# A fused attention and FFT-mixing kernel on one core: its instruction list laid out with other durations, and three small moves of work

## The chip, the cores and the metric

The kernel runs on one core of one Trainium2 chip. The metric is device time in microseconds from launch to end; a profiled execution has a span of its own, from the first to the last instruction. A core has the engines TensorE (PE in the profile), VectorE (DVE), ScalarE (ACT), GpSimd (POOL) and SyncE (SP, which here issues all transfers).

## The reference

For 8 batches of 8 heads: 32 global queries attend to all 544 keys, 512 local queries attend to the 32 global keys and to local keys at most 32 away. The result `x` (8 x 544 x 512) goes through a mixing layer with two weights, 512x2048 and 2048x512:

```python
X = np.fft.fft(np.fft.fft(x, axis=1), axis=2)
u = x + np.real(X)
un = (u - mu) / np.sqrt(var + 1e-06)       # over the last axis
out = u + np.maximum(un @ w_ch1, 0.0) @ w_ch2
```

The inputs are float32 and the weights come as 64-bit floats' bits. All products are made of float16 high and low parts (three matmuls for one product).

## The kernel before

**A list made by a planner.** All work is a list of jobs. `jobs_...` methods add jobs to a `Plan`: an engine, an estimated duration in us, a method that emits the instructions, what it reads and writes, and perhaps a due time `t`. `Plan.targets` gives the other jobs due times backwards from their successors; `Plan.run` simulates five engines, at each step starting on an engine the ready job with the earliest due time. `emit` then writes the instructions in that order. On the chip each engine takes its own in order and waits for semaphores, so the estimates change nothing but the order. Buffers are rings (`X` 3, `uh` 2, `ph` 3, `pl` 3, `h` 3, `ps1` 2, `acc0`, `acc1`, `un`, `lw` 1) and a pool of four PSUM banks; the order of the list decides who gets a free one.

**The weights.** 32 tiles are loaded (`w_load`, L401); POOL (or ACT, each `ALOW`-th) makes a piece of the low bits (`w_low`, L417, L415), ACT scales the high word (`w_split64`, L408), DVE joins them (`w_size`, L421, and `w_sign`, L435), TensorE adds up magnitudes by block (`w_sum`, L431, into `acc0` or `acc1`), DVE takes a maximum of each block of four tiles (`w_max`, L441) and a power of two as scale. Then `w_hi` (ACT, L471) makes the float16 high part and `w_lo` the low part: on DVE in one instruction (L464), or, for the tile numbers in `LOP`, on POOL in two (L461, L462). `W_AT`, `W_PACE`, `W2_AT`, `S_AT`, `S2_AT` and so on are due times.

**Attention.** A batch has four pairs of heads `p`, a pair four units `u`. A pair's `load` and `load_v` may start at `hold` (`L_HOLD` for batches after the first) and, with `queue`, when the simulated transfer queue is nearly empty. `sums` and `sums_v` (ACT, L520) are block sums for a scale; `z_total`, `z_scale` follow. `prep_...`, `v_...` split queries, keys and values into high and low parts. Then for each unit: `scores` (PE, L616), `masked` (DVE, L624), `exps` (ACT, L631), `p_hi` (ACT, L635), `p_lo` (POOL, L640), `turn` (SP, a DMA transpose, L645), `values` (PE, L661, L664), and `norm` for two units (DVE, L675 to L677), which writes `X`. `U_AT`, `B_AT` and `APER` are the due times of a pair's scores in `unit_at`; `EARLY` is the number of pairs with early estimates for PE.

**The DFT of a batch.** DVE and POOL fold rows and columns (`d_odd`, `d_even`, `d_even2`, `d_odd2`, L808 to L847, `d_tail` on POOL), ACT and DVE split the result (`d_hi`, L855, `d_lo`, L859, `d_tail_hi`, `d_tail_lo`, L882), `d_first` is the first DFT (PE, L905; five tiles, for batch 0 in the PSUM tiles that `SPARE` names), `d_z`, `d_z2` split again, `d_second` (L940) is the second DFT, and `d_add`, `d_addc` (DVE, L966, L957), `d_as`, `d_tadd` (L972, L977 to L980) add it to `X`.

**The FFN.** 17 chunks of 256 rows, two halves `j` each. Before a chunk: `l_bn`, `l_v` (DVE statistics), `l_un` (DVE, L1019, normed rows in float32, tile `un`), `l_hi` (ACT, L1023), `l_lo` (DVE, L1027), `l_turn` (SP, L1033, into `uh`). Then for eight `fp`: `f_first` (PE, L1059, into `ps1`), `f_hi` (ACT, L1064), `f_lo` (DVE, L1068), `f_second` (PE, L1078). FFN matmuls have the latest due times on PE, so that they fill what attention and DFT leave. `l_root` is on POOL. Chunks 13 to 16 run as two pairs (`jobs_duo`) with seven products in place of eight for the first layer (L1207, L1273); POOL and ACT prepare mixed weights for them (`jobs_mixes`, `t_sum`, L1108, to `t_lo`, L1129).

The functions that the change touches:

## Time and profile before

| | |
|---|---|
| time, median of 3 runs | 1028.36 us (1025.35 to 1030.54) |
| the profiled execution | 1025.88 us, span 1024.1 us |
| PE busy | 920.3 us (90%) |
| DVE busy | 733.5 us (72%) |
| ACT busy | 611.5 us (60%) |
| POOL busy | 599.1 us (59%) |
| mean granted TensorE clock | 0.939 |

A busy share is an average over stages that differ; the page cuts the span into 40 slices of 25.6 us, and a table by stage gives each engine's busy time in a stretch that one names. A granted clock of 1.00 is 2.4 GHz, one of 0.50 is 1.2 GHz. Lines (L640) are those of the kernel printed above.

### The profile page before, as it was taken

What the parts mean: (1) busy time and instruction counts of PE and PEld (TensorE: products, weight loads), DVE (VectorE), ACT (ScalarE), POOL (GpSimd) and SP (SyncE); (2) the same over time, 40 slices, a digit from 0 to 9 for tenths busy, and PEclk for the clock granted to TensorE, in tenths of its full rate; (3) what the DMA queues carried; (4) which work ended last, traced back from release to release, by engine and by line L of the source; (5) the groups of instructions that cost most, each with busy time, mean ns of one, the idle gap of its engine ahead of it and who ended that gap; (6) DMA issues with size and microseconds to landing.
All of it is one profiled execution on the core that took longest, in us unless ns stands there. A gap on an engine that the chain in (4) does not pass through costs nothing. (4 is left out here: it accounts for less than half of the span.)

```text
span 1024.1 us, 25350 instructions
## 1 busy us (share of the span) xinstructions
PE 920.3 (90%) x9768; PEld 641.4 (63%) x9768; DVE 733.5 (72%) x1929; ACT 611.5 (60%) x1347; POOL 599.1 (59%) x861
## 2 busy tenths in 40 slices
PE   2354459999999999999999999999999999899996
PEld 1233347667667767676776676677766775566663
DVE  4887999977668756785688567956775678975543
ACT  7996769973687478637864886487446344312210
POOL 6999856872587168616962785476436598711000
PEclk9555569999999999999999999999999999999998
DMA  9899456462575276327752865367226213112001
GB/s 364 250 280 235 110 107 134 105 148 42 129 148 130 46 156 151 87 55 146 136 129 46 142 154 99 84 122 140 41 58 107 55 22 68 39 27 78 1 1 41
DMA packets 227809, 113.10 MB, mean 110 GB/s; under 512 B 202824, under 2 KB 210152, under 8 KB 227688
## 3 DMA queue, kind: packets, MB, share of 16 engines
q1 hardware_dynamic: 227688, 111.49, 48.4%
q8 instruction: 76, 1.25, 0.5%
q14 instruction: 45, 0.37, 0.1%
HBM read 47.37 MB, written 9.44 MB: 55 GB/s over the span
## 5 line engine op out<-in xcount | busy, mean ns | idle before, releaser
L1059 PE MATMUL ps<-uh,wh 128*128 128x256 f16 x2496 | 291.4, 274 | 0.9 <-DMA uh<-unh 0.9
L1078 PE MATMUL acc<-wh,h 128*128 128x512 f16 x1248 | 287.6, 381 | 0.5 <-DVE h L1068 0.5
L1059 PEld LDWEIGHTS <-wh 128*128 128x128 f16 x2496 | 240.8, 98 | 36.3 <-issue 2.0
L1078 PEld LDWEIGHTS <-h 128*128 128x128 f16 x1248 | 116.9, 98 | 129.6 <-issue 2.3
L640 POOL TENSOR_TENSOR ph<-pe,ph 128x448 f16<-128x448 f32 (+1 forms) x128 | 139.9, 1107 | 77.7 <-ACT ph L635 57.4
L1068 DVE SCALAR_TENSOR_TENSOR h<-ps,h 128x512 f16<-128x512 f32 x104 | 71.5, 687 | 102.2 <-ACT h L1064 102.0
L1064 ACT ACTIVATE h<-ps 128x512 f16<-128x512 f32 x104 | 61.6, 592 | 112.0 <-PE ps L1059 111.5
L624 DVE CUSTOM_DVE_ANT_0 pe<-bk,msk,z 128x224 f32<-128x224 f32 (+1 forms) x256 | 102.4, 454 | 24.0 <-PE bk L616 20.7
L631 ACT ACTIVATE pe<-pe,nm 128x224 f32<-128x224 f32 (+1 forms) x256 | 105.0, 476 | 13.1 <-DVE nm L624 12.9
L661 PE MATMUL bk<-vN,pl 128*128 128x65 f16 x768 | 67.0, 201 | 21.9 <-DMA pl<-ph 13.6
L635 ACT ACTIVATE ph<-pe 128x448 f16<-128x448 f32 (+1 forms) x128 | 70.7, 579 | 18.6 <-DMA pl<-ph 17.9
L1039 POOL TENSOR_TENSOR ve<-ve 128x2 f32<-128x2 f32 x17 | 4.3, 255 | 120.8 <-DVE un L1019 99.7
L661 PEld LDWEIGHTS <-pl 128*128 128x128 f16 x768 | 59.4, 103 | 24.1 <-DMA pl<-ph 18.7
L664 PEld LDWEIGHTS <-pl 96*128 96x128 f16 (+1 forms) x768 | 57.4, 103 | 9.8 <-issue 5.7
L616 PEld LDWEIGHTS <-qT 64*128 64x128 f16 x1536 | 49.8, 98 | 21.9 <-issue 18.2
L616 PE MATMUL bk<-kT,qT 64*128 64x192 f16 (+2 forms) x1536 | 57.1, 220 | 6.8 <-POOL kT L600 4.2
L664 PE MATMUL bk<-vB,pl 96*128 96x65 f16 (+1 forms) x576 | 51.6, 202 | 0.0
L431 PE MATMUL wl<-wm,partb 128*128 128x256 bf16 x64 | 18.6, 394 | 32.9 <-DVE wm L421 32.9
L1273 PE MATMUL acc<-wh,h 128*128 128x512 f16 x192 | 46.5, 379 | 1.8 <-DVE h L1260 0.9
L600 POOL TENSOR_TENSOR kT<-qk,kT 128x559 f16<-128x559 f32 x32 | 40.6, 1269 | 12.6 <-ACT kT L595 12.2
L575 POOL TENSOR_TENSOR vN<-vf,vN 128x640 f16<-128x640 f32 x32 | 44.6, 1394 | 5.4 <-ACT vN L571 5.0
L1255 ACT ACTIVATE hb<-ph 128x512 f16<-128x512 f32 x16 | 10.1, 630 | 62.8 <-DVE ph L1240 62.8
(258 smaller groups left out, 1886.7 us busy)
## 6 DMA issues: line engine op xcount, KB each, us to landing
qk<-in_qk SPq DMA_DIRECT2D x32, 535.5 KB
rw<-in_moe_w_ch SPq DMA_DIRECT2D x22, 512.0 KB
vf<-in_v SPq DMA_DIRECT2D x32, 320.0 KB
out<-X SPq DMA_DIRECT2D x13, 512.0 KB
raw<-in_moe_w_ch SPq DMA_DIRECT2D x10, 512.0 KB
vB<-vN SPq DMA_DIRECT2D x32, 97.5 KB
vB<-vN SPq DMA_DIRECT2D x64, 32.5 KB
pl<-ph SPq DMA_TRANSPOSE x128
```

Source lines behind the costliest of these rows:

```text
L616: nc.tensor.matmul(S[h][:, t + w0:t + w1], qT[r, a, j], kT[r, k0:k0 + w1 - w0], start=m == 0, stop=m == 2)
L624: nc.vector.tensor_tensor_reduce(self.per[j][:, h, 0:w], S[h][:, t:t + w], self.msk[:, j, 0:w], z[:, 8:9], 3e38, op0=ALU.add, op1=ALU.min, ...
L631: self.nc.scalar.activation(pe[:, h], pe[:, h], AF.Exp, bias=nm[:, h:h + 1], scale=-1.0)
L635: self.nc.scalar.activation(ph[:, 0, :, 0:WIDE[i % 4]], self.per[i % 4][:, :, 0:WIDE[i % 4]], AF.Copy)
L640: self.nc.gpsimd.tensor_sub(ph[:, 1, :, 0:w], self.per[i % 4][:, :, 0:w], ph[:, 0, :, 0:w])
L661: nc.tensor.matmul(pv[:, j % 2, h], pl[:, 4 * a + 2 * h], vN[:, j, c, h, :], start=m == 0, stop=False)
L664: nc.tensor.matmul(pv[:, j % 2, h], pl[0:n, 4 * a + 2 * h + 1], vb, start=False, stop=m == 2)
L1059: nc.tensor.matmul(ps[:, q], wt[:, w, c0:c0 + P], uh[:, :, 4 * a + kt, :], start=n == 0, stop=n == 11)
L1064: self.nc.scalar.activation(h[:, 0], self.fps[c, fp], AF.Relu)
L1068: self.nc.vector.scalar_tensor_tensor(h[:, 1], self.fps.pop((c, fp)), 0.0, h[:, 0], op0=ALU.max, op1=ALU.subtract)
L1078: nc.tensor.matmul(self.acc_f[c][j], h[:, a, q, j * P:(j + 1) * P], self.w[1, f][:, w, :], start=f == 0 and a == 0 and w == 0, stop=f == 1 ...
L1273: nc.tensor.matmul(self.acc_f[c][j], h[:, a, q, j * P:(j + 1) * P], self.w[1, f][:, w, :], start=first and q + a + w == 0, stop=last and q ...
```

## The change

Estimated durations and due times of many jobs are replaced, so the list has another order. Beside that, this work itself changes: `LOP` is empty, so all `w_lo` are on DVE; `l_hi` makes the high part from `X` with a scale and a bias and not from `un`, and half 1's `un` lies in the tile `lw`; `d_odd2` is cut into `d_odd1` and `d_odd2`; batch 0's first DFT takes other PSUM tiles (`SPARE`); the mixed weights wait for `ht` of batch 7; and three tail jobs of the last batch's DFT get their due times 40 us earlier like the rest (`BOOST`). Loads of later batches are held until 90 in place of 50, scores of later batches are due from 140 at 103 us a batch in place of 150 at 109. `warm` adds no job, since `WARM` is empty.

```diff
...
 PERIOD = 109.0
-U_AT, U_PACE = 9.0, 4.0
-B_AT, B_PACE = 150.0, 5.0
-W_AT, W_PACE = 7.0, 2.6
+U_AT, U_PACE = 12.0, 4.5
+B_AT, B_PACE = 140.0, 5.0
+W_AT, W_PACE = 4.0, 2.2
 W2_AT, W2_PACE = 48.0, 2.6
-S_AT, S_PACE = 25.0, 4.2
-S2_AT, S2_PACE = 190.0, 5.0
+S_AT, S_PACE = 40.0, 3.2
+S2_AT, S2_PACE = 190.0, 4.0
...
 ALOW = 4
-LOP = (1, 3, 5, 7, 9, 11, 13, 15)
-EARLY = 6
-L_HOLD = 50.0
-QUEUE = 4.0
+LOP = ()
+EARLY = 4
+WARM = ()
+L_HOLD = 90.0
+QUEUE = 2.0
...
 LNB = True
-SPARE = {0: "acc0", 1: "acc1", 4: "ps1", 2: "ps1", (0, 0): "acc0", (0, 1): "acc1"}
+SPARE = {0: "ps1", 1: "ps1", 4: "acc0", (0, 0): "acc0", (0, 1): "acc1"}
...
 MATE = {c: (u, n) for u, v in enumerate(PAIRS) for n, c in enumerate(v)}
-APER = 109.0
+APER = 103.0
...
     def emit(self):
+        t0 = min(j.start for j in self.order if j.fn.__name__ == "f_first")
         for j in self.order:
+            if j.fn.__name__ == "warm" and j.start > t0:
+                continue
...

+    def d_odd1(self, b):
+        self.odd_rows(self.nc.vector, self.D[b]["s4"][:, :, P:2 * P])
+
...
         se, s4 = self.nc.vector, self.D[b]["s4"]
-        self.odd_rows(se, s4[:, :, P:2 * P])
...
         L = self.L[c]
-        L["un", j] = un = self.p1.tile([P, DM], F32, name="un", tag="un")
-        L["hl", j] = hl = self.p2.tile([P, 2, DM], F16, name="unh")
+        L["un", j] = un = self.p1.tile([P, DM], F32, name="un", tag=("un", "lw")[j])
...
         L = self.L[c]
-        self.nc.scalar.activation(L["hl", j][:, 0], L["un", j], AF.Copy)
+        L["hl", j] = hl = self.p2.tile([P, 2, DM], F16, name="unh")
+        ve = L["ve"]
+        self.nc.scalar.activation(hl[:, 0], self.u_row(c, j), AF.Identity, scale=ve[:, 1, j:j + 1], bias=ve[:, 2, j:j + 1])
...
             add("ACT", .55, self.w_split64, k, i, r=[raw], w=[w, m], k=x4, t=T + .5)
-            add("DVE", .62, self.w_size, k, i, r=[m, lw], w=[w], t=T + 1.5)
+            add("DVE", .66, self.w_size, k, i, r=[m, lw], w=[w], t=T + 1.5)
...
             add("PE", .52, self.w_sum, k, i, r=[w], w=[wl] + end, t=T + 2)
-            add("DVE", .62, self.w_sign, k, i, r=[m, w], w=[w], t=T + 2)
+            add("DVE", .66, self.w_sign, k, i, r=[m, w], w=[w], t=T + 2)
...
             else:
-                add("DVE", 1.15, self.w_lo, k, i, False, r=[w], w=[h], t=T + 1)
+                add("DVE", .92, self.w_lo, k, i, False, r=[w], w=[h], t=T + 1)
+
+    def warm(self, n):
+        self.nc.tensor.matmul(self.bank(("bank", "wm", n)), self.c1[:, 0, 0, 0:P], self.c2.rearrange("p a b c d -> p (a b c d)")[:, 0:512], start=True, stop=True)
+
+    def jobs_warm(self, add):
+        n = 0
+        for count, us, hold in WARM:
+            for _ in range(count):
+                add("PE", us, self.warm, n, r=[("const",)], w=[("bank", "wm", n)], t=1e6, hold=hold, margin=.1)
+                n += 1
...
                 pe, ph = ("pe", u), ("ph", u)
-                add("DVE", .77, self.masked, u, r=[*S, z, ("msk",), pe], w=[pe, ("nm", u)])
+                add("DVE", .92 if p < 8 else .84, self.masked, u, r=[*S, z, ("msk",), pe], w=[pe, ("nm", u)])
...
                 add("POOL", 1.08, self.p_lo, u, r=[pe, ph], w=[ph])
-                add("SP", 1.45, self.turn, u, r=[ph], w=[("pl", u)], svc=1.0, margin=SPM)
+                add("SP", 1.45, self.turn, u, r=[ph], w=[("pl", u)], svc=1.6, margin=SPM)
...
             add("PE", rate * .85, self.g_scores, g, r=[gT] + kv, w=S + [("pg", g)], t=(U[0] + U[2]) / 2, margin=pem)
-            add("DVE", 1.03, self.g_max, g, r=[*S, zg], w=[("ng", g)])
+            add("DVE", 1.1, self.g_max, g, r=[*S, zg], w=[("ng", g)])
...
     def jobs_dft(self, add, b):
-        rate, pem = (PEF, PEM0) if b == 0 else (1.0, PEM)
+        rate, pem = (1.1, PEM0) if b == 0 else (1.0, PEM0 if b == B - 1 else PEM)
...
             add(eng, us, self.d_odd, b, i, r=src, w=[s4h[i]] + ([] if i else [s4]), k=[X, s4])
-            add("DVE", 3.0 if i else 2.9, self.d_even, b, i, r=src, w=[x4h[i]] + own, k=[X, e4])
-        add("DVE", 1.35, self.d_even2, b, r=x4h, w=x4h, k=[e4])
-        add("DVE", 2.3, self.d_odd2, b, r=s4h, w=s4h, k=[s4], late=6.0)
+            add("DVE", 3.25, self.d_even, b, i, r=src, w=[x4h[i]] + own, k=[X, e4])
+        add("DVE", 1.5 if b else 2.6, self.d_even2, b, r=x4h, w=x4h, k=[e4])
+        add("DVE", 1.3, self.d_odd1, b, r=s4h[1:], w=s4h[1:], k=[s4], late=4.0)
+        add("DVE", .95, self.d_odd2, b, r=s4h, w=s4h, k=[s4], late=5.0)
...
             add("ACT", .63, self.d_hi, b, i, r=[*src, dsc], w=[eh[i]], k=own)
-            add("DVE", .70, self.d_lo, b, i, r=[*src, dsc, eh[i]], w=[eh[i]], k=own)
+            add("DVE", .95, self.d_lo, b, i, r=[*src, dsc, eh[i]], w=[eh[i]], k=own)
         add("ACT", 1.48, self.d_tail_hi, b, r=[et, dsc], w=[ht])
-        add("DVE", 1.10, self.d_tail_lo, b, r=[et, dsc, ht], w=[ht])
+        add("DVE", 1.2 if b else 1.7, self.d_tail_lo, b, r=[et, dsc, ht], w=[ht])
...
         for j in range(2):
-            un, hl = ("un", c, j), ("unh", c, j)
-            add("DVE", .58, self.l_un, c, j, r=r0[j:j + 1] + [ve], w=[un, hl], k=[X], t=L, back=LNB)
-            add("ACT", .55, self.l_hi, c, j, r=[un], w=[hl], t=L, back=LNB)
+            un, hl = (("un", "lw")[j], c, j), ("unh", c, j)
+            add("ACT", .60, self.l_hi, c, j, r=r0[j:j + 1] + [ve], w=[hl], k=[X], t=L, back=LNB)
+            add("DVE", .58, self.l_un, c, j, r=r0[j:j + 1] + [ve], w=[un], k=[X], t=L, back=LNB)
...
     def jobs_mixes(self, add):
-        late = [("xM", 31), ("xgo", 7, 1)]
+        late = [("xM", 31), ("xgo", 7, 1), ("ht", 7)]
...
             self.jobs_duo(add, u)
+        self.jobs_warm(add)
...
             n = j.fn.__name__
-            if n.startswith("d") and j.a[0] == B - 1 and not (n in ("d_second", "d_addc", "d_add") and j.a[1] or n in ("d_tailsec", "d_as", "d_tadd")):
+            if n.startswith("d") and j.a[0] == B - 1 and not (n in ("d_second", "d_addc", "d_add") and j.a[1]):
...
```

## Rows read from the trace of the kernel before

**Rows 1.** The page, 40 slices: busy tenths of TensorE

```profile
PE   2354459999999999999999999999999999899996
```

**Rows 2.** Stage table: busy PE, PEld, DVE, ACT, POOL (count); PEclk, DMA, GB/s

```profile
20.00:110.00 90.00, 44.42 (x592) 30.04 (x591) 73.46 (x198) 79.13 (x170) 83.64 (x92) 0.57 0.93 256
110.00:146.00 36.00, 13.69 (x157) 10.58 (x157) 34.89 (x84) 25.57 (x57) 26.22 (x40) 0.59 0.45 99
...
217.00:221.00 4.00, 1.67 (x32) 1.22 (x23) 0.82 (x3) 1.36 (x5) 3.46 (x5) 0.83 0.96 198
221.00:850.00 629.00, 627.85 (x7038) 442.94 (x7037) 449.19 (x1232) 390.98 (x870) 374.27 (x551) 1.00 0.50 100
850.00:900.00 50.00, 45.06 (x305) 30.18 (x304) 43.31 (x83) 16.79 (x37) 39.19 (x56) 0.97 0.26 60
```

**Rows 3.** Timeline of PE: start, us, line, tile, count, idle before

```profile
145.86 5.28 PE L1059 MATMUL ps<-uh,wh 128*128 128x256 f16 x24 [0.92 <-DMA uh<-unh]
```

**Rows 4.** SyncE's waits, 20 to 110 us: us, times, longest

```profile
SPq L645 <- POOL lw L417: 10.4, 5, 4.4
SPq L645 <- POOL wm L461: 4.7, 4, 2.3
```

**Rows 5.** Groups of POOL by line, 20 to 110 us: busy, mean ns, idle

```profile
L461 POOL TENSOR_SCALAR wm<-wm,wsc 128x512 f32<-128x512 f32 x8 | 13.4, 1673 | 0.5
L462 POOL TENSOR_TENSOR wh<-wm,wh 128x512 f16<-128x512 f32 x8 | 9.7, 1211 | 0.7
```

**Rows 6.** Stage table of DVE's L464 alone

```profile
20.00:110.00 90.00, 6.93 (x8) 0.57 0.93 256
```

**Rows 7.** Timeline of DVE, 24 to 142 us

```profile
24.14 1.15 DVE L464 SCALAR_TENSOR_TENSOR wh<-wm,wsc,wh 128x512 f16<-128x512 f32 x1
...
94.38 2.48 DVE L829 TENSOR_TENSOR e<-e 128x128 f32<-128x128 f32 x1
96.77 0.28 DVE L830 TENSOR_TENSOR e<-e 128x128 f32<-128x128 f32 x1
...
109.78 0.42 DVE L677 TENSOR_TENSOR X<-bk,dn 128x256 f32<-128x256 f32 x1
...
124.37 0.41 DVE L441 TENSOR_REDUCE mx<-wl 128x1 f32<-128x256 f32 x1
...
126.13 0.15 DVE L529 TENSOR_SCALAR wsc<-wsc 128x1 int32<-128x1 int32 x1
...
138.41 0.69 DVE L1027 TENSOR_TENSOR unh<-un,unh 128x512 f16<-128x512 f32 x1
...
141.17 0.68 DVE L1027 TENSOR_TENSOR unh<-un,unh 128x512 f16<-128x512 f32 x1
```

**Rows 8.** Stage table of ACT's L520 alone

```profile
20.00:110.00 90.00, 11.17 (x30) 0.57 0.93 256
```

**Rows 9.** Timeline of POOL, 95 us

```profile
95.45 1.25 POOL L808 TENSOR_TENSOR s<-X 128x508 f32<-128x508 f32 x1
```

**Rows 10.** Timeline of ACT, 137 us

```profile
137.74 0.63 ACT L1023 ACTIVATE unh<-un 128x512 f16<-128x512 f32 x1 [0.32 <-DVE un L1019]
```

**Rows 11.** Timeline of ACT, 219 us

```profile
219.75 0.58 ACT L635 ACTIVATE ph<-pe 128x448 f16<-128x448 f32 x1 [2.64 <-DMA pl<-ph]
```

**Rows 12.** Timeline of PE, 888 to 919 us

```profile
888.79 0.80 PE L1207 MATMUL bk<-pe,tq 128*128 128x256 f16 x3 [2.54 <-DVE xt L980]
...
918.36 2.13 PE L1207 MATMUL bk<-pe,tp 128*128 128x256 f16 x18
```

**Rows 13.** Timeline of DVE, 822 us

```profile
822.05 1.52 DVE L882 SCALAR_TENSOR_TENSOR ht<-et,dsc,ht 32x513 f16<-32x513 f32 x1 [0.93 <-ACT ht L878]
```

**Rows 14.** Timeline of POOL, 813 to 898 us

```profile
813.05 2.50 POOL L1108 TENSOR_TENSOR tf<-wh 128x512 f32<-128x512 f16 x2
...
895.99 1.60 POOL L1129 TENSOR_TENSOR tp<-vf,tp 128x512 f16<-128x512 f32 x1
```

## The prediction

> **What bounds the kernel now.** I read the page's row of TensorE first, then the stage table, then what the slow stage waits for. From the seventh slice on TensorE runs at nine tenths or more in all slices but three near the end [rows 1], and from 221 to 850 us it is busy 627.85 of 629 [rows 2]. So nothing but TensorE sets the length of that stretch, and what DVE, ACT or POOL gain or lose there costs nothing unless it opens a hole. What can be won lies at three places: the start, up to the first layer's first matmuls at 145.86 [rows 3]; a hole at 217 to 221 (4.00 - 1.67 = 2.33 us idle); and 850 to 900 (50 - 45.06 = 4.94 us idle) [rows 2]. Of the start, 20 to 110 us is the attention of batch 0 together with splitting the weights, 110 to 146 its DFT and layer norm.
>
> From 20 to 110 us POOL is the fullest engine, 83.64 of 90 us, against ACT 79.13 and DVE 73.46; the DMA share is 0.93 [rows 2]. That POOL is also the one waited for shows in SyncE's own waits: the transposes of attention probabilities (L645) wait 10.4 us that are put down to POOL's weight pieces (L417) and 4.7 us to the first half of a POOL `w_lo` (L461) [rows 4], and SyncE issues in order, so loads stand behind them. From 110 to 146 DVE is the bound: 34.89 of 36 us [rows 2].
>
> The sum is made against the profiled execution, 1025.88 us (span 1024.1). The median of the three runs, 1028.36, is 2.48 above it; I carry the difference over.
>
> **The change part by part.**
>
> *A. Eight `w_lo` from POOL to DVE.* Removed from POOL: 8 x (1.673 + 1.211) = 23.07 us, all between 20 and 110 [rows 5]; POOL falls to 60.6 of 90. Added to DVE: 8 of L464, 8 x 0.866 = 6.93 us by the mean of the eight that DVE has there already [rows 6], so DVE rises to 80.4. One took 1.15 [rows 7], so 9.2 us is the upper bound. The next limits are then DVE 80.4, ACT 79.1 and the DMA queues, 0.93 x 90 = 83.7. The later loads (hold 50 to 90) push block sums of batch 1 out of this stretch: L520 is 11.17 us in 30 instructions there [rows 8], six a pair, so 2.2 us a pair; the two pairs of batch 0 left need 4.5, and 6.7 us can go. That lowers ACT to about 72.5 and takes the same pairs' loads from the queues. So DVE's 80.4 is the floor. The stretch can shrink by 0 (dependences, not POOL, hold it) to 90 - 80.4 = 9.6 us; I take the middle, **-5**: POOL was packed to 93% with SyncE waiting on it, and DVE will not pack better. Queued behind a `w_lo` on DVE is the next masked-scores instruction, and behind that ACT's exponentials; that is why I don't take the full 9.6.
>
> DVE and POOL do slow each other: L829, 128x128, took 2.48 us and ended at 96.86, just when POOL's 1.25 us L808 of 95.45 was over, while L830 of the same shape took 0.28 right after [rows 7, 9]. The Trainium skill, SBUF — State Buffer, "Who interferes with whom", says that a DVE instruction with two SBUF inputs and a POOL instruction that reads SBUF exclude each other. L464 has two such inputs, so the rule speaks against the move: by it POOL would get back only 23.07 - 6.93 = 16.1 us, which leaves it at 67.5 of 90, still below DVE; the sum would be the same.
>
> *B. Layer norm and the first DFT.* `l_hi` now reads X itself with scale and bias on ACT, in place of waiting for `l_un`; it stays one ACT instruction (0.63 us before [rows 10]) and runs beside `l_un`. For row 1 of a chunk `un` gets a tile of its own. Before, un of row 1 had to wait for lo of row 0 (138.41, 0.69), and lo of row 1 came at 141.17 [rows 7]. With both un early, lo of row 1 can follow at about 139.1: 2.07 us for the second transpose, on which the first matmuls wait; bounds 0 to 2.1, taken 2.0. The first DFT's tiles 0 and 1 go to the first layer's PSUM tiles, off those of the weights' block sums, whose last maximum came at 124.37 in the middle of the DFT; its chain on DVE to the last scale ends at 126.28, 1.9 us [rows 7]. It needn't stand there any more: 0 to 1.9, taken 1.0. One DFT tile more takes one of four banks; the scores of batch 1 that then wait are not urgent. The split of `d_odd2` and the new durations can put the even half's low part ahead of odd work: DVE's total is unchanged, so 0 up to the 1.9 of the same place again, taken 1.0 for TensorE and ACT working earlier beside it. Sum **-4.0** (0 to -5.9).
>
> *C. The hole at 217.* ACT stood 2.64 us before L635 for a transpose [rows 11], the second layer waited behind it, and TensorE's granted clock was 0.83 there [rows 2]. The list now counts 1.6 us of queue for each such transpose in place of 1.0. That may or may not move it: 0 to -2.33, and as much again for the low clock; **-1.5**. Against this, attention asked for sooner (103 in place of 109 us a batch) puts more of it ahead of FFN work; bounded by more such holes of 2.33 us in the later batches, taken nothing, since DVE, ACT and POOL are each under 72% busy from 221 to 850 [rows 2].
>
> *D. The end.* The last batch's tail second step and additions (`d_tailsec`, `d_as`, `d_tadd`) are brought forward. TensorE waited 2.54 us for L980, the last of them, at 888.79 [rows 12], and the stretch's clock was 0.97 for 50 us, 1.5 us more [rows 2]. Early, the bank is free long before: 0 to -4.0, taken **-3**. The mixes on POOL now wait for `ht` of batch 7, which was ready at 823.6 (L882) [rows 13] where the first mix had begun at 813.05: 10 us later. Their last instruction ended at 897.59 [rows 14] and what they make last is first used at 918.36 [rows 12]: 20.8 us of cover, so nothing; with the cover gone it would cost the 10 us.
>
> *Back.* A start 9 us shorter has less room for batch 1's TensorE work, which is then done under load. TensorE was busy 13.69 of 36 us at a clock of 0.59 [rows 2], 0.22 us of full-speed work a us: **+2.0** for A and B's 9 us.
>
> *Nothing:* `warm` (its list is empty); the margins, rates and other estimates, which act through the order alone; `QUEUE` 2 lets loads be issued later, and its cover is a queue that is 0.93 busy [rows 2]; where it drains, a load's wait is A's lower bound, nothing gained.
>
> Sum: -5 - 4 - 1.5 - 3 + 2 = -11.5, so 1025.88 - 11.5 = 1014.4 as a profiled execution, and 1028.36 - 11.5 = **1016.9 us** as the median.
>
> **The rivals.**
>
> 1. *The list moves little.* ACT at 79.1 and the queues at 0.93 were nearly as full as POOL; A gives nothing, B and D half (-3.5), C nothing: about 1025. For it: 73.46 + 6.93 on DVE is only 3 us under POOL's 83.64. Against: SyncE's waits name POOL, not ACT or DVE [rows 4].
> 2. *All covers hold.* A -9.6, B -5.9, C -4.7, D -4.0, back +3.5: -20.7, 1007.7. Against: DVE would have to be packed without a gap from 20 to 110 us.
> 3. *Slower: DVE becomes the bound of the start.* The eight `w_lo` fall due among the masked scores and before the DFT. Once DVE is the engine on which 20 to 110 us ends, each us put on it is a us of the span: 8 x 1.15 = +9.2, B and D at half, -3.5: 1034. It decides from the point where DVE has under 7 us of idle time before the first DFT; it had 16.5 [rows 2].
> 4. *Slower: the steady stretch gets holes.* Attention asked for 6 us a batch sooner stands in the in-order queues of ACT and SyncE ahead of FFN's `f_hi`. A hole like that at 217, with its low clock 3.5 us, in each of seven batches is +24.5, less 11.5: 1041; it turns the sign from four such holes on.
>
> **How the numbers follow.** My forecast (1010 to 1022) 0.50; rival 1, 0.22; rival 2, 0.12; rivals 3 and 4, 0.16 together, a quarter of it near the old time. A measurement here can tell about 0.5% (5.1 us) from no change: faster is under 1023.2, slower over 1033.5. Faster: 0.50 + 0.12 + a small part of rival 1, 0.64. Same: the rest of rival 1 and the quarter, 0.24. Slower: 0.12. The range takes in rivals 1 and 2 with a little beside them and leaves out most of 3 and 4: 1006 to 1031; the likeliest case alone is 1010 to 1022.
>
> **What would show it.** A: no L461 or L462 on POOL; POOL under 75% busy up to the last attention norm of batch 0, and that norm, at 109.78 before [rows 7], ahead of 106. B: the hi rounding beside un, the first matmul of the first layer between 134 and 140. C: TensorE without a hole over 2 us from there to 850. D: no wait for the tail's additions. I am wrong if the first layer still starts at 145 or later (rivals 1, 3), or if TensorE idles more than 5 us in the steady stretch (rival 4).

## The result, and the profile after

The changed kernel takes **1017.92 us** (median of 4 runs, 1017.44 to 1018.22) against 1028.05 for the kernel before (4 runs beside it, 1025.35 to 1030.54): a ratio of 0.9902, 95% interval 0.9876 to 0.9927. The forecast was 1016.9, range 1006 to 1031, likeliest case 1010 to 1022. Its profiled execution took 1017.78 us with a span of 1016.0, against 1025.88 and 1024.1: 8.1 us less, where the sum of the prediction had 11.5. All medians, ranges and ratios here and below leave out one execution of run 10 (3245 us) and one of the kernel before beside runs 5 to 8 (2391 us), which ran in a slow state.

The total came out near the forecast. Its parts did not, and alone, in the old order, none of those tried is worth anything.

The stage table of the changed kernel answers to [rows 2] ("..." marks what is left out). Columns as there: stretch, its length, busy time of PE, PEld, DVE, ACT, POOL, then PEclk, DMA share, GB/s. The second stretch ends where the first layer now begins.

```profile
20.00:110.00 90.00, 44.18 (x588) 30.51 (x587) 84.34 (x206) 76.35 (x163) 68.66 (x83) 0.60 0.89 244
110.00:143.00 33.00, 12.28 (x107) 9.19 (x107) 26.46 (x63) 22.70 (x47) 16.37 (x29) 0.55 0.34 98
143.00:217.00 74.00, 73.88 (x951) 53.24 (x948) 66.46 (x174) 68.12 (x152) 59.13 (x78) 0.99 0.72 134
217.00:221.00 4.00, 4.00 (x32) 2.81 (x30) 3.86 (x8) 2.01 (x4) 4.00 (x5) 1.00 0.64 166
221.00:825.00 604.00, 603.53 (x6920) 430.66 (x6919) 446.51 (x1233) 397.85 (x870) 364.94 (x541) 1.00 0.53 106
221.00:850.00 629.00, 626.59 (x7079) 446.05 (x7078) 470.96 (x1278) 406.54 (x888) 387.76 (x580) 1.00 0.53 105
...
825.00:850.00 25.00, 23.06 (x162) 15.39 (x160) 24.46 (x46) 8.70 (x18) 22.82 (x40) 1.00 0.42 92
...
850.00:900.00 50.00, 45.39 (x309) 29.58 (x308) 44.08 (x75) 16.02 (x36) 35.70 (x53) 1.00 0.23 41
```

Rows of the kernel before are needed beside it that the prediction did not use: its first layer's first 71 us, the 4.3 us behind the hole, and the stretch up to 850 us in two parts.

```profile
146.00:217.00 71.00, 71.00 (x896) 51.35 (x896) 61.51 (x162) 62.38 (x140) 53.77 (x71) 0.96 0.57 127
...
219.70:224.00 4.30, 4.29 (x23) 2.09 (x24) 3.16 (x5) 4.16 (x10) 3.69 (x7) 0.61 0.81 141
221.00:825.00 604.00, 602.85 (x6834) 426.00 (x6832) 428.87 (x1199) 381.78 (x852) 351.34 (x528) 1.00 0.51 103
825.00:850.00 25.00, 25.00 (x206) 16.93 (x205) 20.32 (x34) 9.21 (x19) 22.93 (x24) 1.00 0.12 23
```

Three things are to be seen. In 20 to 110 us POOL fell from 83.64 to 68.66 and DVE rose from 73.46 to 84.34; DVE is now the fullest engine. In 110 to 143 us no engine is full: DVE, the bound of that stretch before (34.89 of 36), is busy 26.46 of 33. And the hole at 217 is gone, with TensorE's granted clock at 1.00 there in place of 0.83 (and of 0.61 from the hole's end to 224), and at 0.99 in place of 0.96 ahead of it.

The timeline of the changed kernel, PE first: the first layer's first matmul is the third row [rows 3].

```profile
119.14 0.42 PE L911 MATMUL dps<-c1r,eh 128*128 128x144 f16 x2 [5.89 <-ACT eh L861]
...
140.18 0.59 PE L459 MATMUL bk<-vac,part 128*128 128x6 f32 x2 [8.03 <-ACT junk L524]
...
143.06 3.11 PE L1066 MATMUL ps<-uh,wh 128*128 128x256 f16 x20
```

DVE, from the last attention norm of batch 0 (L681) to the layer norm's low parts (L1034) [rows 7]:

```profile
105.79 0.42 DVE L681 TENSOR_TENSOR X<-bk,dn 128x256 f32<-128x256 f32 x1
...
117.63 0.75 DVE L888 SCALAR_TENSOR_TENSOR ht<-et,dsc,ht 32x513 f16<-32x513 f32 x1 [5.00 <-ACT ht L884]
...
121.06 0.42 DVE L445 TENSOR_REDUCE mx<-wl 128x1 f32<-128x256 f32 x1
...
136.34 1.00 DVE L1024 TENSOR_SCALAR un<-X,ve 128x512 f32<-128x512 f32 x2
137.26 1.33 DVE L1034 TENSOR_TENSOR unh<-un,unh 128x512 f16<-128x512 f32 x2
```

And ACT in the same stretch; L524 is a block sum of batch 1, L884 and L861 are the first DFT's roundings, L1030 the layer norm's high part:

```profile
109.36 0.74 ACT L524 ACTIVATE junk<-vf 128x640 f16<-128x640 f32 x1 [2.11 <-DMA vf<-in_v]
...
114.47 0.63 ACT L524 ACTIVATE junk<-qk 128x512 f16<-128x512 f32 x1 [1.88 <-DMA qk<-in_qk]
...
116.88 1.47 ACT L884 ACTIVATE ht<-et,dsc 32x513 f16<-32x513 f32 x2
118.36 0.72 ACT L861 ACTIVATE eh<-e,dsc 128x514 f16<-128x514 f32 x1
...
136.34 1.52 ACT L1030 ACTIVATE unh<-X,ve 128x512 f16<-128x512 f32 x2 [2.92 <-DVE ve L1019]
```

The norm came 3.99 us earlier (109.78 to 105.79), the first matmul only 2.80 (145.86 to 143.06): on the way 1.2 us were lost, not 4 won. The place is in the rows. DVE stands 5.00 us for a rounding on ACT, and ACT, which takes its work in order, stood 2.11 and 1.88 us for loads of batch 1 whose sums are listed ahead of that rounding. TensorE's 5.89 us ends on the same work.

### The profile page after: what moved, and what is told of

It reads as the page before. It is cut to its first block, busy times and chain, and to the rows that moved or that the text cites. A ratio compares the mean times of both kernels' runs of the same rounds, so it can differ in the third digit from the quotient of the medians.

```text
span 1016.0 us, 25330 instructions
## 1 busy us (share of the span) xinstructions
PE 915.6 (90%) x9768; PEld 641.7 (63%) x9768; DVE 754.4 (74%) x1937; ACT 620.2 (61%) x1347; POOL 581.4 (57%) x845
## 4 chain that ended last, share of the span: by engine, by line
PE 76%; DVE 13%; ACT 4%; issue 3%; DMA 3%; POOL 1%; SPq 0%; DVEq 0%; ACTq 0%; POOLq 0%
PE ps L1066 24%; PE acc L1085 24%; PE bk L1214 6%; PE ps L1280 4%; PE bk L620 4%; PE acc L1280 3%; PE bk L665 2%; PE bk L668 2%; PE bk L911 1%; PE bk L946 1%; PE bk L692 1%; PE bk L728 1%; DVE unh L1172 1%; DVE wm L425 1%; DVE wm L439 1%
## 5 line engine op out<-in xcount | busy, mean ns | idle before, releaser
L1262 ACT ACTIVATE hb<-ph 128x512 f16<-128x512 f32 x16 | 10.1, 630 | 70.8 <-DVE ph L1247 70.8
L568 POOL TENSOR_TENSOR vf<-vf,z 128x640 f32<-128x640 f32 x32 | 41.7, 1302 | 16.4 <-DVE ge L530 13.0
L524 ACT ACTIVATE junk<-qk 128x512 f16<-128x512 f32 x64 | 41.4, 647 | 8.0 <-DMA qk<-in_qk 6.7
```

## The experiments

Lines in kernels with inserted code are shifted by a few. "Norm" is the last attention norm of batch 0, "matmul" the first of the first layer, both from the profiled execution; the time is the median with its range, the ratio is the recorded one, to the kernel before in the same round, whose median was 1028.05 beside runs 1 to 4, 1027.4 beside 5 to 11 and 1027.06 beside 12. So times of different rounds can't be compared to better than 1 us.

| run | norm | matmul | time, us | ratio (95%) |
|---|---|---|---|---|
| before | 109.78 | 145.86 | 1028.05 (1025.35 to 1030.54) | |
| after | 105.79 | 143.06 | 1017.92 (1017.44 to 1018.22) | 0.9902 (0.9876 to 0.9927) |
| 1 after, two loads earlier | 105.91 | 139.43 | 1016.00 (1014.42 to 1016.72) | 0.9876 (0.9849 to 0.9903) |
| 2 after, eight `w_lo` on POOL | 113.07 | 147.57 | 1023.02 (1022.05 to 1025.28) | 0.9950 (0.9932 to 0.9968) |
| 3 before, eight `w_lo` on DVE | 110.72 | 147.07 | 1028.70 (1027.41 to 1030.19) | 1.0010 (0.9996 to 1.0025) |
| 4 after, edits of the end undone | 105.89 | 142.23 | 1017.57 (1017.05 to 1017.69) | 0.9894 (0.9864 to 0.9925) |
| 5 before, loads later | 110.54 | 146.90 | 1029.08 (1026.43 to 1032.78) | 1.0022 (1.0002 to 1.0042) |
| 6 before, 3 and 5 together | 110.08 | 146.38 | 1026.72 (1024.37 to 1029.17) | 0.9989 (0.9972 to 1.0006) |
| 7 after, old transpose price | 108.29 | 145.18 | 1018.18 (1017.53 to 1019.18) | 0.9919 (0.9897 to 0.9941) |
| 8 after, start reordered | 105.64 | 137.36 | 1016.57 (1015.98 to 1018.32) | 0.9905 (0.9882 to 0.9929) |
| 9 the same, again | 106.28 | 138.87 | 1019.15 (1017.37 to 1021.62) | 0.9913 (0.9883 to 0.9942) |
| 10 as 9, warm matmuls | 105.77 | 138.54 | 1019.69 (1018.40 to 1021.32) | 0.9925 (0.9902 to 0.9947) |
| 11 after, layer norm undone | 106.20 | 144.93 | 1025.75 (1022.36 to 1027.93) | 0.9984 (0.9965 to 1.0002) |
| 12 before, layer norm alone | 109.43 | 145.30 | 1027.57 (1025.09 to 1032.54) | 1.0001 (0.9985 to 1.0018) |

**1. Two loads earlier.** Between the two small transfers of `x_mid` SyncE stands until the first has come through; two loads of batch 1 go into that gap. The order of all other work stays.

```diff
         self.nc.sync.dma_start(self.cols(self.X[b][0:1, 3], g), t)
+        if g == 1:
+            self.load_v(4)
+            self.load_v(5)
         self.nc.sync.dma_start(t, self.cols(self.xd[0:1], g))
```

> The changed kernel, its list kept, but for two loads of batch 1's values: SyncE issues them between the two small transfers of the attention's last rows, where it stood 2.8 us, and not behind the second. Theory (ACT, in order, stands before batch 1's block sums for late loads, and the first DFT's roundings stand behind them): ACT's wait of 2.11 us before the first of these sums goes, the wait of 1.88 us shrinks, the DFT's first rounding (L884) moves from 116.88 to 112.5 to 114, the first layer's first matmul from 143.06 to 139 to 141, the time from 1017.9 to 1014 to 1016. Rival (the roundings are not what is late; the last weights' maximum, the layer norm or the transposes are): L884 earlier, but the first matmul within 0.7 us of 143.06 and the time within 1 us of 1017.9. Second rival (the loads delay the small transfer, and so the DFT's tail): L884 at 117 or later, 1018 to 1021.

ACT's two waits are gone, and the roundings and the first matmul moved by 3.8 and 3.63 us. ACT and PE of this run:

```profile
113.07 1.47 ACT L889 ACTIVATE ht<-et,dsc 32x513 f16<-32x513 f32 x2
114.55 0.72 ACT L866 ACTIVATE eh<-e,dsc 128x514 f16<-128x514 f32 x1
```

```profile
139.43 6.74 PE L1071 MATMUL ps<-uh,wh 128*128 128x256 f16 x48
```

The theory held: what step B lost on the way was ACT standing in order before the loads that the change had moved there. The profiled execution is 3.4 us shorter (span 1012.6); the median is 1.9 shorter, with all four runs below the four of the changed kernel, though the two intervals overlap. It has the lowest median of the study.

Run 4 below, whose list is the same up to 688 us, bears the theory out without any edit at this place: the second load happened to come sooner, ACT waited 0.97 us for it in place of 1.88, and the rounding (116.05) and the first matmul (142.23) were both 0.83 us earlier. ACT of run 4:

```profile
113.65 0.63 ACT L524 ACTIVATE junk<-qk 128x512 f16<-128x512 f32 x1 [0.97 <-DMA qk<-in_qk]
...
116.05 1.47 ACT L884 ACTIVATE ht<-et,dsc 32x513 f16<-32x513 f32 x2
```

It also shows how far one profiled execution differs from another at the first matmul: differences under about 0.8 us are not to be read. By run 4 the way from the norm lost 0.3 us and not 1.2; that it did not win 4 holds by either.

**2 and 3. The eight `w_lo` by themselves**, in either list, each in its place.

```diff
     def w_lo(self, k, i, pool):
         f, s, w = self.wf.pop((k, i))
-        if pool:
+        if k == 0 and (4 * (i % 4) + i // 4) % 2:   # run 2, in the changed kernel
+        if False:                                   # run 3, in the kernel before
```

> The changed kernel, its list kept, with the eight low halves of weights back on POOL, each in its place in the list. Theory (step A: POOL sets the length of 20 to 110 us): POOL is busy 83 or more of 90 us there, the last attention norm of batch 0 moves from 105.79 to 109 to 111, the first layer's first matmul by 3 to 5 us, the time to 1021 to 1023. Rival (the new order made the gain, not the engine): norm within 1.5 us of 105.79, time 1017 to 1019.5. Second rival (this list, laid out for an empty POOL, falls apart with the eight on it): norm later than 113, time above 1025.

> The kernel before, its list kept, with nothing changed but that the eight low halves of weights run on DVE in one instruction each, in their old places. Theory (step A alone, -5): the last attention norm of batch 0 from 109.78 to 104 to 107, the first layer's first matmul from 145.86 to 141 to 143, time 1028 to 1023 to 1025. Rival (it needs the new order as well; DVE's masked scores queue behind the eight): norm within 1.5 us of 109.78, time 1026.5 to 1029. Third (DVE becomes the bound): norm at 111 or later, above 1029.

Undone in the new list, the step costs 7.3 us at the norm, 4.5 us at the first matmul and 5.1 us of time. The time is the prediction's 5, but the norm at 113.07 came later than the theory's 109 to 111 and passed the mark of the second rival, a list that falls apart with the eight on POOL (the time above 1025 that it also asked for was not there). So the 5.1 us are the price of the eight in a list made without them. Done alone in the old list, it gives nothing. The stage row and the norm of run 3, then SyncE with two of its waits in 20 to 110 us, then ACT, where the kernel before's line stands first:

```profile
20.00:110.00 90.00, 43.03 (x590) 29.86 (x589) 79.71 (x203) 77.82 (x168) 61.33 (x75) 0.56 0.94 257
```

```profile
110.72 0.42 DVE L677 TENSOR_TENSOR X<-bk,dn 128x256 f32<-128x256 f32 x1
```

```profile
85.70 0.76 SPq L755 DMA_DIRECT2D X<-xt  x1
91.00 0.59 SPq L756 DMA_DIRECT2D xt<-xd  x1
```

```profile
SPq L645 <- POOL ph L640: 7.0, 4, 2.7
...
SPq L645 <- POOL lw L417: 5.9, 4, 3.0
```

```profile
99.20 0.58 ACT L635 ACTIVATE ph<-pe 128x448 f16<-128x448 f32 x1 [4.64 <-DMA pl<-ph]
...
100.16 0.58 ACT L635 ACTIVATE ph<-pe 128x448 f16<-128x448 f32 x1 [5.05 <-DMA pl<-ph]
```

POOL gave up 22.3 us (83.64 to 61.33), just the 23 that were counted, and the norm came 0.9 us later. SyncE issues the small transfer at 85.70 and the one behind it 5.3 us later, and ACT then stands 5.05 us for a transpose that is queued behind both. In the kernel before that wait was 4.64 us. So the eight `w_lo`, though named in SyncE's waits of the old list [rows 4], were not what held it: with them taken away, the same SyncE order ran to nearly the same times, and its waits were put down to other POOL work, 7.0 us to `p_lo` (L640) and still 5.9 to L417. That POOL's remaining work holds it is not excluded.

**5 and 6. Is it the queue?** Two loads of batch 1 (`load_v` of pairs 4 and 5) are issued some 10 us later in the old list, with the sums that read them behind.

```diff
+MOVE = (
+    (('load_v', 4), ('turn', 12)),
+    (('load_v', 5), ('load_v', 4)),
+    (('sums_v', 4), ('p_hi', 15)),
+    (('sums', 5, 'q'), ('sums_v', 4)),
+    (('sums', 5, 'k'), ('sums', 5, 'q')),
+    (('sums_v', 5), ('sums', 5, 'k')),
+)
...
+        for one, to in MOVE:
+            order.remove(at[one])
+            order.insert(order.index(at[to]) + 1, at[one])
```

> The kernel before, its list kept, but for two loads of batch 1's values, which SyncE issues about 10 us later, behind the transposes of batch 0's thirteenth unit, with the four block sums that read pair 4's and 5's rest behind them on ACT. Theory (the queues: SyncE stands before the second small transfer of the attention's rows, L756, until the first has come through behind bulk loads, and the transposes behind it stand too): the sixth attention norm of batch 0 moves from 101.47 to 97 to 100, the last from 109.78 to 106 to 108, the first layer's first matmul from 145.86 to 142 to 144, time 1024 to 1026.5. Rival (POOL, still with its eight low halves, sets this stretch): the sixth norm within 1.5 us, time 1027 to 1029.5.

> As the run with the loads later in the kernel before's list, and the eight low halves of weights on DVE as well. Theory (the eight are worth something only where the queues no longer hold SyncE): the last norm 103 to 106, 2 us or more ahead of the run with the loads alone, time 1021 to 1024. Rival (in this list the engine of the eight doesn't matter at all; the gain of the changed kernel is that of its order): within 1 us of the run with the loads alone. Second rival (neither matters): time 1027 to 1029.5.

My theory of the queue fell. The gap between the issues of the two small transfers shrank, from 2.9 us in the kernel before to 1.8 in run 5 (86.84 to 88.63), and from 5.3 in run 3 to 3.4 in run 6; the sixth norm came at 100.18 and 99.87 against 101.47, but the last norm at 110.54 and 110.08, no earlier than before. ACT's wait for the transpose did not shrink: 4.64 us in the kernel before and 5.05 in run 3, 4.83 in run 5, and in run 6:

```profile
97.61 0.58 ACT L649 ACTIVATE ph<-pe 128x448 f16<-128x448 f32 x1 [5.16 <-DMA pl<-ph]
```

Run 5 alone has its rival's numbers, by which POOL with the eight sets the stretch; run 6, without the eight, speaks against that as well. Both moves together are at most 0.3% better than the kernel before, and the interval holds no change. What in the old order holds 20 to 110 us stays open: with both moves DVE is busy 80.34, ACT 79.44 of 90 us and the DMA share is 0.92, and no single one of these was shown to be it.

**4. The end.** Both edits of step D undone; the list is the same up to 688 us.

```diff
-        late = [("xM", 31), ("xgo", 7, 1), ("ht", 7)]
+        late = [("xM", 31), ("xgo", 7, 1)]
...
-            if n.startswith("d") and j.a[0] == B - 1 and not (n in ("d_second", "d_addc", "d_add") and j.a[1]):
+            if n.startswith("d") and j.a[0] == B - 1 and not (n in ("d_second", "d_addc", "d_add") and j.a[1] or n in ("d_tailsec", "d_as", "d_tadd")):
```

> The changed kernel with the two edits of the end undone: the last batch's tail second step and additions have their old due times, and the mixes on POOL don't wait for the tail's rounding of batch 7. The list is the same up to 688 us. Theory (step D, -3): the wait of 2.5 us for the tail's addition is back, time 1020 to 1022. Rival (the end is bound by DVE, and the edits gave nothing): TensorE idle 825 to 900 us 5.5 to 7.5, time 1017 to 1019. Second rival (the edits cost time, since the mixes now run against DVE's layer-norm pieces of the last chunks): idle under 5, time 1014.5 to 1016.5.

The first rival held: 1017.57, and TensorE idle 5.46 us in 825 to 900, at the lower edge of what it had named. Both edits were undone at once, so the two are not told apart. TensorE's waits behind 700 us in this run, engine and line, releaser, us in total, times, longest:

```profile
PE acc L1280 <- ACT h L1262: 3.2, 2, 2.6
PE bk L1214 <- DVE msk L1249: 1.9, 1, 1.9
PE bk L1214 <- DVE xt L986: 0.3, 1, 0.3
```

Against them, the changed kernel's own, from 143 us on (behind 700 us the second line reads 1.9, 2, 1.6, the others are the same):

```profile
PE bk L1214 <- DVE msk L1249: 2.9, 2, 1.9
PE acc L1085 <- DVE h L1075: 2.4, 3, 1.6
PE acc L1280 <- DVE h L1267: 1.7, 2, 1.4
```

The wait for the tail's last addition (L986; L980 before, 2.54 us in [rows 12]) is only 0.3 us even without the edits, in the new order. In either version TensorE waits for other outputs of DVE or ACT there, with DVE busy 24.46 of 25 us in 825 to 850.

**7. The price of a transpose.** The whole list is laid out anew with the old 1.0.

```diff
-                add("SP", 1.45, self.turn, u, r=[ph], w=[("pl", u)], svc=1.6, margin=SPM)
+                add("SP", 1.45, self.turn, u, r=[ph], w=[("pl", u)], svc=1.0, margin=SPM)
```

> The changed kernel with the old queue price of a transpose of probabilities, 1.0 for 1.6 us, in the costs from which the list is laid out; the whole list is laid out anew. Theory (step C, -1.5: that price took away the hole at 217): TensorE stands 2 us or more at once before the transposes' reader somewhere between 143 and 400 us, and the time is 1019 to 1022. Rival (the hole was a chance of the old list, and went with any new order): no such hole, time 1016.5 to 1019.

The stage table of this run, in the place of the old hole:

```profile
217.00:230.00 13.00, 13.00 (x107) 8.67 (x106) 12.64 (x29) 9.21 (x20) 8.64 (x11) 1.00 0.53 144
```

TensorE is busy 13.00 of 13 us at a clock of 1.00: no hole, the rival. Run 9, on the other hand, has a wait of 2.6 us for such a transpose with the price at 1.6. So the price did not decide it: whether there is a hole differs from order to order. Run 7 shows more: its first matmul, at 145.18, is 2.1 us later than the changed kernel's, and its time is the same within 0.3 us. It idles nothing in 221 to 825 and 4.25 us in 825 to 900 (0.47 and 6.55 in the changed kernel).

**8, 9 and 10. A start reordered by hand.** Between 101 and 145 us, work that is not due goes behind the first layer norm; run 9 puts right what run 8's order had made wait; run 10 adds matmuls that nobody reads. In both orders one load (`load_v` of pair 4) stands in the gap of `x_mid`. The core of run 9's moves, each "this, behind that", and run 10's addition:

```diff
+MOVE = (
+    (('load', 5), ('x_mid', 1)),
+    (('w_sign', 1, 15), ('d_odd1', 0)),
+    (('sums', 6, 'q'), ('prep_hi', 5, 'q')),
...
+    (('z_total', 2), ('d_first', 0, 3)),
+    (('d_z2', 0, 3), ('d_z2', 0, 2)),
+    (('d_addc', 0, 0), ('d_z2', 0, 3)),
...
+    (('w_lo', 1, 0, False), ('d_add', 0, 1, 1)),
...
+    (('v_out', 4), ('l_turn', 0, 1)),
...
+    (('f_first', 0, 0), ('w_lo', 1, 1, False)),
...
+    (('scores', 8), ('z_total', 3)),
+    (('f_hi', 0, 0), ('scores', 8)),
+    (('f_lo', 0, 0), ('l_bn', 1, 1)),
+)
...
     def d_tailsec(self, b):
         for cs in range(2):
             self.d_second(b, 2, cs)
+        if b == 0:
+            wm = self.ps.tile([P, 512], F32, name="wm", tag="acc1")
+            for _ in range(14):
+                self.nc.tensor.matmul(wm, self.c1[:, 0, 0, 0:P], self.c2.rearrange("p a b c d -> p (a b c d)")[:, 0:512], start=True, stop=True)
```

> The changed kernel with its list reordered by hand between 101 and 145 us: the small transfers of the attention's last rows ahead of the loads of batch 1; pair 6's block sums, the second layer's first weight pieces and batch 1's first scores behind the first layer norm; the weights' last sign step ahead of the DFT's roundings and their last maximum behind them. Theory (the stretch 106 to 143 is a chain through small instructions that stands behind work that is not due): the DFT's first rounding of the tail (L884 of the changed kernel) at 110 to 112.5, the first layer's first matmul at 133 to 137, time 1011 to 1014.5. Rival (a floor of the chain itself, above all the small transfers and the transposes): first matmul within 1.5 us of 139.43, that of the run with two loads moved. Second rival (what the start gains comes back, since the work put off is done under load): first matmul 3 us earlier, time within 1 us of 1016.0.

> The reordering of the start once more, with what the first try left standing put right: the odd part's last z piece right behind the one before it on DVE, pair 6's block sums where ACT stood idle for 3.4 us, the weights' last maximum in its old place, and the first layer's first rounding (ACT) and its low part (DVE) ahead of the second chunk's layer norm. Theory (each of the first try's stalls was of my order's making): first layer's first matmul at 134 to 136, no wait of 2 us for that rounding, time 1012 to 1014.5. Rival (work that is put off comes back under load, DVE and ACT being 0.9 busy behind the start): first matmul as early, time 1015 to 1017.

> The same order with 14 matmuls of 512 columns more, into a PSUM tile that nobody reads, behind the first DFT's last matmul, where TensorE stood idle for some 8 us before the first layer. Theory (the first layer's first matmuls run at the low clock level because TensorE stood idle before them): granted clock above 0.9 in the first 5 us of the first layer, against 0.5 to 0.6, and 1.5 to 2.5 us less than the same order without them. Rival (the clock is low for another reason, or what it gives is taken by waits for the roundings): less than 0.7 us.

All three theories failed. Run 8 has its first matmul 2.1 us ahead of run 1 and is not faster, nearest to its second rival: TensorE then stood 2.43 us for the first layer's first rounding, which ACT took behind the second chunk's layer norm. Run 9 has its first matmul at 138.87, where 134 to 136 was expected. It has its batch statistics done at 127.86, 2.7 us ahead of run 1's, and lost them at once; DVE, then POOL, in run 9:

```profile
127.90 1.24 DVE L1049 TENSOR_SCALAR ve<-mv 128x2 f32<-128x2 f32 x1
129.17 1.17 DVE L1050 TENSOR_SCALAR ve<-ve 128x2 int32<-128x2 int32 x1
130.37 1.07 DVE L1051 SCALAR_TENSOR_TENSOR ve<-mv,ve 128x2 f32<-128x2 f32 x1
131.48 2.19 DVE L1056 TENSOR_SCALAR un<-X,ve 128x512 f32<-128x512 f32 x2
```

```profile
127.76 1.35 POOL L609 TENSOR_TENSOR vN<-vf,vN 128x640 f16<-128x640 f32 x1
129.07 1.25 POOL L634 TENSOR_TENSOR kT<-qk,kT 128x559 f16<-128x559 f32 x1
130.27 1.16 POOL L634 TENSOR_TENSOR qT<-qk,qT 128x512 f16<-128x512 f32 x1
```

Three instructions of two columns took over 1 us each, and each ends within 0.04 us of a POOL instruction's end (129.14 and 129.11, 130.34 and 130.32, 131.44 and 131.43). In run 1 the same lines took 0.34, 0.54 and 1.17 us, and the two `un` behind them 1.00 for 2.19; so both runs have the first low part at the same time, 133.59 and 133.62. Run 9 is no faster than the changed kernel; that it is slower, by 1.2 us of the medians, is not shown, since its executions range from 1017.37 to 1021.62. The first low part on DVE, which I had put forward, stood 3.89 us with other work behind it, for a rounding on ACT that itself stood 3.18 us for the first matmuls, and TensorE idled 3.20 us in 143 to 217, against 0.12. Run 10's matmuls gave nothing: they ended at 130.8, TensorE then stood 7.71 us, and the granted clock in 140 to 145 us was 0.65 against 0.55 in run 9, where above 0.9 was expected: a mix of the two levels in both. Matmuls up to the first layer's start were not tried.

**11 and 12. The layer norm by itself.** Run 11 undoes it in the changed kernel, with row 1's `un` and high part issued behind row 0's low part; run 12 does it alone in the kernel before, with row 1's behind row 0's. Both keep the rest of their list. The diff is run 11's, without the lines that move the jobs; run 12 has these lines the other way round.

```diff
     def l_un(self, c, j):
...
-        L["un", j] = un = self.p1.tile([P, DM], F32, name="un", tag=("un", "lw")[j])
+        L["un", j] = un = self.p1.tile([P, DM], F32, name="un", tag="un")
...
     def l_hi(self, c, j):
...
-        self.nc.scalar.activation(hl[:, 0], self.u_row(c, j), AF.Identity, scale=ve[:, 1, j:j + 1], bias=ve[:, 2, j:j + 1])
+        self.nc.scalar.activation(hl[:, 0], L["un", j], AF.Copy)
```

> The changed kernel, its list kept, but for the layer norm of the chunks: the high half on ACT reads un again and waits for it, and both rows of a chunk share one tile un, so that row 1's un stands behind row 0's low part. Theory (step B, 2.0 of its 4.0): row 1's low part 1.5 to 2.1 us later against its first batch statistics, the first layer's first matmul from 143.06 to 144.5 to 145.2, time 1019 to 1020.5. Rival (the second transpose is not what the first matmuls wait for, or the steady stretch hides it): first matmul within 0.7 us, time within 0.8 us of 1017.9.

> The kernel before, its list kept, with the layer norm's part of the change alone: the high half on ACT reads X with scale and bias, both rows of a chunk have a tile un of their own, and row 1's un and high half are issued right behind row 0's. Theory (the layer norm's term of step B, 2.0 at the start, and nothing else): the first layer's first matmul from 145.86 to 143.6 to 144.6, time 1028 to 1025.5 to 1027. Second theory (what the run without it lost, 7.8 us, is its worth in any order, by holes in the steady stretch too): time 1020 to 1023.5. Rival (in a list laid out for the old layer norm nothing is gained, since transposes and loads stand in SyncE's old order): first matmul within 0.7 us of 145.86, time within 1.5 us of 1028.

Undone, it costs 1.87 us at the first matmul, as the theory said (0.41 of it stands at the norm already), but 7.8 us of time, which neither the theory nor the rival had. The rest is behind the start; PE of run 11 in 230 to 825 us, where the changed kernel idles 0.47:

```profile
230.00:825.00 595.00, 590.48 (x6812) 421.56 (x6811) 434.31 (x1217) 387.73 (x862) 353.14 (x532) 1.00 0.51 105
```

It idles 4.52 us there, in waits of the second layer for ACT and DVE and of the attention for a transpose. Alone in the old list it gives nothing. DVE of run 12 shows why at the start:

```profile
138.32 0.69 DVE L1034 TENSOR_TENSOR unh<-un,unh 128x512 f16<-128x512 f32 x1
138.92 1.66 DVE L972 SCALAR_TENSOR_TENSOR X<-bk,dsc,X 128x256 f32<-128x256 f32 x4
140.49 0.68 DVE L1034 TENSOR_TENSOR unh<-un,unh 128x512 f16<-128x512 f32 x1
```

Both rows could be ready together, but the kept order has four additions of the second chunk between their low parts. The second came at 140.49 for 141.17.

## Why the prediction came out as it did

| step | predicted | seen in the traces |
|---|---|---|
| A, start up to the norm | -5 | -4.0 |
| B, norm to first matmul | -4 | +1.2 (+0.3 in run 4) |
| C, hole at 217 | -1.5 | -4.0 (2.33 idle, 4.3 x 0.39 of clock behind it) |
| clock, first layer to 217 | not in the sum | -2.1 (71 x 0.04 less 74 x 0.01) |
| D, the end | -3 | +0.1 (idle -0.33 in 850 to 900, +1.94 in 825 to 850, clock -1.5) |
| 221 to 825 | 0 | -0.7 |
| back | +2.0 | +1.4, what is left |
| sum | -11.5 | -8.1 |

The clock column has two digits, and 0.01 of 71 us is 0.7 us; the last lines are no finer than that.

*A.* The norm came 4.0 us earlier, and the step cost 5.1 us of time when undone in place, so the size was near. From 20 us to the norm's end at 106.2 DVE is busy 80.78 us, as the text had it (80.4), packed to 93.7%; POOL stood at 77.0% where the text said under 75, and ACT at 74.80 us for 72.5, since 18 of the 30 block-sum instructions stayed and not 12. What failed is the reading under it, that SyncE's waits for POOL [rows 4] mean that POOL's load sets the stretch. Run 3 took 22.3 us off POOL and nothing moved. The step has its worth only together with the rest of the new order. Rival 1, that ACT and the queues were nearly as full as POOL, fits what runs 3, 5 and 6 show of the old order, but which of them holds it was not shown. And rival 3's turning point, under 7 us idle on DVE, was crossed (5.43) without its loss.

*B.* The sign named for it, a first matmul between 134 and 140, was missed: 143.06. The layer norm's term was right: 2.0 foreseen, 1.87 when undone. The step that failed is in A's working: "the later loads push block sums of batch 1 out of this stretch". Twelve instructions did go, into the next, ahead of the DFT's roundings on an engine that takes its work in order, and before loads that land late. I took their going for a gain and never asked where they would stand. Run 1 measures it: 3.6 us. With that taken off, the way from the norm is 2.6 us shorter than before, so the two other terms, the PSUM tiles and the split of `d_odd2`, are worth some 0.7 us together and not 2.0 (a size within the scatter of single executions). "It needn't stand there any more", said of the weights' last maximum, failed too: at 121.06 it still stands between the DFT's steps.

*C.* The hole went, and is worth more than was taken, since the clock was low behind it, up to 224. The price of 1.6, to which the step was put down, did not do it (run 7).

*D.* The wait for the tail's addition went, but not by the edits (run 4), and waits for DVE took its place: -3 became about nothing. The sign that the prediction had named, no wait for the tail's additions, was there, and yet D gave nothing: it asked for the old wait alone and not for what is late next.

*Not in the sum.* The first layer's first 71 us ran at 0.96 before and at 0.99 after. Before, the granted clock was 0.50 up to 150 us, 4.1 us behind the first matmul, and 0.65 in 150 to 152; after, it was 0.59 in 143 to 145 and 1.00 from there. Ahead of the first matmul TensorE now works on scores of batch 1 from 140.70 on, with one gap of 0.73 us; before, it had stood 7.76 us up to 141.30, and 0.69 and 0.92 us behind that. Whether this is why the clock rose sooner was not tested.

*The whole.* Parts were costed one by one and added. Run 3 and run 12 give 0 for A and the layer norm alone; run 2 and run 11 give 5.1 and 7.8 for the same two undone, 12.9 together, more than the 10.1 that the whole change is worth. In this list, laid out as one, these parts have no price of their own. The new order by itself, laid out with the eight on POOL and the old layer norm, was not tried, so its share of the 10.1 us stays open.

The prediction also looked for most of its gain in the wrong place: 9.0 us at the start, less 2.0 back, where 2.8 were found, less 1.4. Run 2 starts its first layer 1.7 us later than the kernel before and is still 5.0 us faster by the medians; run 7 starts it at 145.18, past the 145 that the prediction took as the sign of being wrong, and is about as fast as the changed kernel. So that sign tells nothing here.

That the total was hit is luck, the sum of errors of both signs: A, B and D fell short by 9.3 us together, C, the clock and the steady stretch gave 5.3 more, and 0.6 less came back. And of the 10.1 us between the medians some 2 are in no step: the profiled execution of the kernel before lay 2.2 us under its median, where four executions spread over 5.2 us, and that of the changed kernel 0.1 under its own.

## What to carry to other kernels

When a change moves work out of a full stretch, write down where each moved instruction stands next, on which in-order engine, and for which transfer it will wait there; that is the price to look for. An engine that is busiest, and named in other engines' waits, is the bound only if the stretch shortens when it is relieved in place, which one run can tell. Where an order is laid out as a whole, test a part both ways, alone in the old order and undone in the new; if the two differ, part and order are worth something only together, and the part's price can't be added to others.

## What was not expected of the hardware

Instructions of two columns on DVE took 1.07 to 1.24 us (run 9), where the same lines of run 12 took 0.52, 0.17 and 0.16, and each ended with a POOL instruction that had begun before it. So tiny steps of a serial chain are the ones to keep clear of POOL's long ones: run 9 lost there what its order had won. The Trainium skill, SBUF — State Buffer, "Who interferes with whom", says that a DVE instruction with two SBUF inputs contends with a GpSimd instruction that reads SBUF, and that one in a mode with two ports contends too: whichever engine issues first gets the shared pair of ports for its whole instruction, and the other waits. These rows agree with it, though no run shows in which mode the two instructions with one input (L1049, L1050) ran. The other way round no such price shows: by the rule the prediction had POOL get back only 16.1 us of the eight `w_lo`, and in run 3 it got back 22.3 of 23.07. That does not refute the rule: POOL was idle for 28.67 of the 90 us there, and the eight need not have met its work.
